# VectorE's order in the second full-attention layer: polynomial steps ahead of side-matmul reads

## The chip, the cores and the metric

The kernel runs on one core of one Trainium2 chip. The metric is the device time of one execution in microseconds (us). The engines that matter here are TensorE (PE in the profile, with PEld for its weight loads), VectorE (DVE), ScalarE (ACT), GpSimd (POOL) and the DMA queue that SyncE (SP) feeds. Each engine works through its own instruction list in order; the lists are tied together by semaphores. In this kernel the lists of TensorE, and in the full layers that of VectorE as well, are written out by hand: the program that builds the kernel decides which instruction stands behind which.

## The reference

Four transformer-like attention blocks follow each other on one sequence of 2048 rows of 512 numbers, with 32 heads of 16: a sliding-window block (window 256), a full block, the same window block again and the same full block again. Each block is

```
x = x + softmax(mask(q k^T / 4)) v  @ wo        with  q, k, v = layernorm(x) @ wqkv
```

The window blocks mask all but the last 256 keys; the full blocks mask nothing, so 32 heads x 2048 x 2048 exponentials are needed in each. The input `x` and the weights are float32 random numbers, scaled by 0.05. The kernel computes this in float32 quality: matrix products are made of float16 pieces (high and low part), and a path of higher safety, which does not run for these inputs, stands behind a flag.

## The kernel before

**Layers.** The layers are numbered 0 to 3. Layers 0 and 2 are window layers, 1 and 3 the full ones. The change concerns layer 3, the second full layer.

**Visits.** A full layer is worked in 32 *visits*. One visit takes four heads (`qd`) and 512 queries (`c`), and goes through the 2048 keys in 16 tiles of 128 keys (`attn_full`, L845). For each tile there are two score matmul sets (L789), one for each pair of heads, each into a bank pair `s` of the accumulator memory (PSUM; two such tiles exist). ScalarE takes the exponential of 1024 columns at once (L801) into `e`, and TensorE multiplies by the values into `acc` (L865), a tile later. In layer 3 the visits come in 16 *groups* of two: a group is one set of 512 queries (`c`) with eight heads (`t`), so `qd = 2t` and then `2t + 1`. In this text visits are counted from 0 to 31, so odd visits are the second ones of their groups.

**VectorE's own exponentials.** In layer 3, VectorE takes a share: in tile 5 (`OWN_J`, L40) of every visit, one of the two heads of each pair is not given to ScalarE (which then runs the half-size form, L798) but to VectorE (`own_exp`, L758). VectorE reads the scores at once (L763, two reads in a visit) and then needs seven further steps for each read: two integer operations (L766, L767) and five of a polynomial (L769). These fourteen steps have no fixed place. They are put in the last of five queues, `VQ[4]`, and go out when the program finds time. When all are out, the value products that need them, the *late halves* (`late`, L871: two sets of TensorE matmuls with `op` as an operand, each over half of the queries), may be issued, one half per tile (L1162), as soon as the planner's clock has passed the modelled end of the last step by 1.0. If the visit's last tile comes before that, both are put behind the last tile's own value product (L880). After it the epilogue (L721) reads `acc`, and the next visit's value products may overwrite it.

**Side work.** Between the tiles stands work that other visits and the layer's end need, the *side work*: projections of queries and keys (`project`, read by VectorE into `j`, L523 and the lines behind), value projections (`vt`), and the output projection (`wo_part`, L703, where VectorE adds two bank halves onto `x`, L717). All side matmuls of a full layer write one bank pair `b`, so the next side matmul must wait until VectorE has read the last. For the bound of the softmax the program also needs sums of squares: GpSimd squares the projection (`sq`, L537), TensorE sums them over a head with a matmul with ones (`squares`, L551; matmul at L559) into the same bank `b`, and VectorE reads that into `m` (queries, L593 and L594) or `km` (keys, L578). Squares that are still owed stand in the list `pend`, and `settle` (L609) issues those whose time has come; it may issue two in a row.

**What sets the order.** While it writes the lists, the program keeps a clock of TensorE (`clock`) and one of VectorE (`vt_`), both in estimated us. `soon` puts VectorE's operations that need no fixed place into the queues `VQ[0]` to `VQ[4]`. `drain` takes from the first queue that has something, as long as VectorE's clock is no more than 0.2 ahead of TensorE's. The fifth queue is skipped when squares are owed, the bank is not in the middle of a product, and the squares can go within 0.9: this is the *hold-back*. `drain(1)` empties only the first queue. `share` (L1053), called for each tile, first looks whether squares may be issued: TensorE's clock must have passed the time they are due, the time at which the bank is free (`PH["free"]`), and VectorE's clock less 0.2. Then it issues side matmuls from a budget. After a side product the bank is called free 2.0 after its last matmul, and the same after squares. A late half puts `PH["free"]` 0.1 past the clock, so that the tile it stands in gets no side matmuls.

```
            if pend and not PH["busy"] and clock[0] >= max(PH["free"], pend[0][0], vt_[0] - 0.2):
                settle(False)
                PH["free"] = clock[0] + 2.0
```

Of the kernel before, what the change touches and what calls it, by code (L numbers as in the profile page):

```python
# [193 lines left out]
def fast_path(ctx, tc, flag, a_x, a_wqkv, a_wo, b_wqkv, b_wo, out):  # L194
# [20 lines left out]
    XC, XN, V, O, OT, KM, PH = {}, {}, {}, {}, {}, {}, {"free": 0.0, "busy": False, "late": None}  # L215
    WT, ST, pend = {}, {}, []
    VQ, vt_ = [deque() for _ in range(5)], [0.0]

    clock, DONE, XNR, ONR = [0.0], {}, {}, {}
# [9 lines left out]
    def vec(us):  # L229

        vt_[0] = max(vt_[0], clock[0]) + us
# [8 lines left out]
    def drain(upto=None):  # L240

        if upto is not None:
            for q in VQ[:upto]:
                while q:
                    vec(q[0][1])
                    q.popleft()[2]()
            return
        while vt_[0] <= clock[0] + 0.2:
            q = next((q for q in VQ[:4 if pend and not PH["busy"] and max(pend[0][0], PH["free"]) <= clock[0] + 0.9 else 5] if q), None)
            if q is None:  # L250
                return
            vec(q[0][1])
            q.popleft()[2]()

    def turns(chain, *ops):

# [237 lines left out]
    def project(l, s, c, act, ht=None, ring=0):  # L494


        ty, n = l % 2, f"{l}_{s}_{c}" + ("" if ht is None else f"_h{ht}")
        w = weights(ty, s, n, *((0, D, 0) if ht is None else (ht * P, (ht + 1) * P, ring)))
        yield wait(8)
        xc = XC[l, c]  # L500
        if s == 0:
            dst = rows(qs[ty, c])
        elif ty == 0:
            dst = rows(kw[c])
        else:
            dst = rows(kf)[:, :, c * QC:(c + 1) * QC]
        sqs = {}
        for t in range(NHT) if ht is None else (ht,):
            ps = bank()
            w0 = t * P if ht is None else 0  # L510
            yield from mms(ps, [(w[:, k, a, w0:w0 + P], xc[:, b, k, :]) for a, b in TERMS for k in range(NC)], 2.2)
            if not PH["full"]:
                settle(not sqs)
            with tc.high_priority(HEAD_START):
                if PH["full"]:
                    drain(1)
                    j = vp.tile([P, QC], F32, name=f"j{n}_{t}", tag="j")
                    join(j, (ps[:, 0], ps[:, 1]))
                else:
                    sp = vp.tile([P, 2, QC], F16, name=f"sp{n}_{t}", tag="sp", bufs=3)  # L520
                    if act:
                        nc.scalar.activation(sp[:, 0], ps, AF.Copy, scale=1 / WS)
                    else:  # L523
                        nc.vector.tensor_scalar(sp[:, 0], ps, 1 / WS, None, op0=ALU.mult)
                    nc.vector.scalar_tensor_tensor(sp[:, 1], ps, 1 / WS, sp[:, 0], op0=ALU.mult, op1=ALU.subtract)
            full = PH["full"]

            def parts(t=t, sp=None if full else sp, j=j if full else None):
                if full:
                    sp = vp.tile([P, 2, QC], F16, name=f"sp{n}_{t}", tag="sp", bufs=3)  # L530
                    nc.vector.tensor_copy(sp[:, 0], j)  # L531
                    nc.vector.tensor_tensor(sp[:, 1], j, sp[:, 0], ALU.subtract)
                sq = vp.tile([P, QC], BF16, name=f"sq{n}_{t}", tag="sq", bufs=NHT)
                if act:
                    nc.scalar.activation(sq, sp[:, 0], AF.Square)
                else:
                    nc.gpsimd.tensor_tensor(sq, sp[:, 0], sp[:, 0], ALU.mult)  # L537
                sqs[t] = sq

                d = dst[8 * t:8 * t + 8].rearrange("h (d b) n -> (h d) b n", b=4)  # L540
                if s:
                    nc.sync.dma_start(d[:, 0:2], sp[:, 0:1].broadcast_to([P, 2, QC]))
                    nc.sync.dma_start(d[:, 2], sp[:, 1])
                else:
                    nc.sync.dma_start(d[:, 0:2], sp)
                    nc.sync.dma_start(d[:, 2], sp[:, 0])
            soon(0, 1.2, parts)
            yield last(MM)
        return sqs

    def squares(n, sqs):  # L551

        drain(1)
        vec(1.4)
        ph = bank()
        for t, sq in sqs.items():
            if PH["full"]:
                for r in range(2):
                    nc.tensor.matmul(ph[32 * t:32 * t + 32, r], hsum[R * r:R * r + R], sq[R * r:R * r + R],  # L559
                                     start=True, stop=True, skip_group_check=True)  # L560
            else:
                nc.tensor.matmul(ph[32 * t:32 * t + 32, :], hsum, sq, start=True, stop=True, skip_group_check=True)
        return ph

    def quarters(ht):
# [137 lines left out]
    def wo_part(c, t):  # L703

        w = wp.tile([P, NC, 2, D], F16, name=f"wo_{c}_{t}", tag="w", bufs=WB)[:, 0]
        nc.sync.dma_start(w, wd[1, 3][:, t])
        xs = load_x(3, c)
        yield wait(4)
        o = O.pop((3, c, t))
        for i in range(4):  # L710
            ps = bank()
            yield from mms(ps, [(o[:, a, i * P:(i + 1) * P], w[:, b, :]) for a, b in TERMS])
            vec(1.4)
            k = 4 * c + i
            with tc.high_priority(HEAD_START):
                for p in ((ps[:, 0], ps[:, 1]) if PH["full"] else (ps,)):
                    nc.vector.scalar_tensor_tensor(xs[i], p, 1 / WS, xs[i], op0=ALU.mult, op1=ALU.add)  # L717
            nc.sync.dma_start(out[0, k * P:(k + 1) * P, :] if t == NHT - 1 else xd[k], xs[i])
            yield -MM
# [266 lines left out]
    class Side:  # L986
# [66 lines left out]
        def share(self):  # L1053

            self.budget = min(self.budget + max((self.cost - self.spent) / max(self.steps - 3 - self.k, 1), self.least), 0.75)
            self.lag = max(self.lag - 0.42, -0.3)
            if pend and not PH["busy"] and clock[0] >= max(PH["free"], pend[0][0], vt_[0] - 0.2):
                settle(False)
                PH["free"] = clock[0] + 2.0
                self.lag += 0.1  # L1060
            s0, most = self.spent, 2.5 * MM if self.more and self.lag < -0.2 and self.budget > 0.7 else 1.5 * MM
            while (self.q and clock[0] >= PH["free"] and self.budget >= MM / 2 and (self.lag < 0.25 or self.budget > 0.45)
                   and self.spent - s0 < most):
                c = self.one()
                if c is None:
                    break
                self.budget -= abs(c)
                self.lag += abs(c)
# [324 lines left out]
```

## Time and profile before

| | |
|---|---|
| median of 3 runs | 2710.74 us (2704.07, 2710.74, 2710.8) |
| the profiled execution | 2705.62 us |
| its span, first to last instruction | 2703.4 us |
| layer 3, from its first exponential to its last | 1711.55 to 2683.3 us |
| ScalarE busy in the whole span | 2350.0 us (87%) |
| TensorE busy in the whole span (its ends are modelled) | 2490.6 us (92%) |
| VectorE busy in the whole span | 1436.0 us (53%) |
| granted clock of TensorE | 0.99 |

The profile is one execution. Its views name an instruction by its line in the kernel, the engine, and the tiles as `out<-in`. In a timeline each row gives the start and the length in us, and in brackets how long the engine had been idle before it and what ended that. A row with `x2` stands for two instructions of one kind in a row. The view of waits sums such idle times: who waited, for whom, us in total, how often, and the longest. `op` is the name of VectorE's exponentials in the late halves, and also that of a tile of the epilogue.

### The profile page before, as it was taken

The page shows a single profiled execution, that of the slowest core. Times are in us where ns is not written, and L with a number is a line of the kernel's source. Part 1 is how long each engine was busy: PE and PEld are TensorE (multiplying, and loading weights), DVE is VectorE, ACT ScalarE, POOL GpSimd, SP SyncE. Part 2 cuts the span into 40 slices and gives each one's busy share as a digit, 9 for nine tenths or more (in the row PEclk, how much of TensorE's full clock was granted, in tenths as well). Part 3 has the DMA queues.
Part 4 walks back from the last instruction along what each step waited for, and adds up shares of the span by engine and source line. Part 5 has one row for each costly group of instructions (what it writes and reads, how often), then busy time and mean ns, then how long its engine had stood idle before and what let it go on. Part 6 is the DMA issues. An engine that isn't in the chain of part 4 may idle for free.

```text
span 2703.4 us, 124036 instructions
## 1 busy us (share of the span) xinstructions
PE 2490.6 (92%) x56047; PEld 1164.5 (43%) x56047; DVE 1436.0 (53%) x2862; ACT 2350.0 (87%) x2671; POOL 549.7 (20%) x1136
## 2 busy tenths in 40 slices
PE   7889999999998999999999999889999999999997
PEld 3344444444443444444444444434444444444442
DVE  5576353223334335334336666466656676677675
ACT  4666765999999999999996775789999999999996
POOL 1556550001000000100116786010000001100000
PEclk9999999999999999999999999999999999999999
DMA  8899875222334325224326656423333333334332
GB/s 282 251 276 267 236 201 150 67 95 91 104 99 120 100 85 153 93 87 114 97 88 206 189 164 168 119 85 105 97 92 96 96 95 111 104 97 133 129 118 93
DMA packets 341204, 361.49 MB, mean 134 GB/s; under 512 B 117800, under 2 KB 256568, under 8 KB 334392
## 3 DMA queue, kind: packets, MB, share of 16 engines
q1 hardware_dynamic: 340664, 353.46, 43.9%
q8 instruction: 440, 7.21, 1.1%
q14 instruction: 100, 0.82, 0.1%
HBM read 240.65 MB, written 96.99 MB: 125 GB/s over the span
## 4 chain that ended last, share of the span: by engine, by line
ACT 51%; PE 28%; issue 11%; DVE 6%; DMA 2%; POOL 1%; SPq 1%; ACTq 0%; DVEq 0%; POOLq 0%
ACT e L801 50%; PE b L409 8%; PE acc L865 5%; PE acc L914 4%; PE s L789 4%; PE s L793 2%; PE b L405 2%; PE bs L412 2%; PE b L412 2%; DMA kt<-kw 1%; DVE xh L464 1%; POOL e L907 0%; DVE xn L458 0%; ACT e L798 0%; DVE xh L458 0%
## 5 line engine op out<-in xcount | busy, mean ns | idle before, releaser
L801 ACT ACTIVATE e<-s 128x1024 f32<-128x1024 f32 (+2 forms) x2368 | 2193.1, 1046 | 165.9 <-PE s L793 104.6
L865 PE MATMUL acc<-e,vt 64*17 64x512 f32 (+1 forms) x17152 | 1112.3, 566 | 0.7 <-issue 0.4
L789 PE MATMUL s<-qt,kt 64*32 64x512 f16 x16384 | 884.5, 381 | 121.4 <-ACT e L801 97.3
L789 PEld LDWEIGHTS <-kt 64*32 64x32 f16 x16384 | 403.5, 89 | 887.3 <-issue 787.6
L865 PEld LDWEIGHTS acc<-e,vt 64*17 64x17 f32 x17152 | 303.5, 92 | 78.1 <-issue 9.3
L907 POOL TENSOR_SCALAR_AFFINE_SELECT e<-e 128x256 f32<-128x256 f32 x512 | 231.2, 459 | 153.5 <-ACT e L801 152.8
L904 POOL TENSOR_SCALAR_AFFINE_SELECT e<-e 128x256 f32<-128x256 f32 x448 | 200.8, 454 | 98.4 <-ACT e L801 95.1
L914 PE MATMUL acc<-e,vt 128*17 128x384 f32 (+2 forms) x2816 | 201.5, 388 | 2.0 <-POOL e L904 1.7
L431 DVE TENSOR_SCALAR sa<-acc 128x512 f32<-128x512 f32 x64 | 44.2, 691 | 287.9 <-PE acc L865 287.9
L409 PE MATMUL b<-xc,w 128*32 128x512 f16 x2496 | 154.5, 392 | 11.8 <-DVE km L578 6.7
L537 POOL TENSOR_TENSOR sq<-sp 128x512 bf16<-128x512 f16 x32 | 45.8, 1434 | 505.3 <-DVE sp L531 482.1
L793 PE MATMUL s<-qt,kt 64*128 64x384 f16 (+2 forms) x1408 | 120.5, 275 | 27.1 <-ACT e L801 21.2
L769 DVE SCALAR_TENSOR_TENSOR op<-op,ou 128x512 f32<-128x512 f32 x192 | 133.4, 695 | 5.8
L431 DVE TENSOR_SCALAR j<-b 128x512 f32<-128x512 f32 x32 | 22.0, 688 | 203.5 <-PE b L405 203.5
L405 PE MATMUL b<-xc,w 64*32 64x512 f16 x3072 | 127.5, 376 | 1.5 <-DVE j L432 0.8
L537 POOL TENSOR_TENSOR sq_h<-sp_h 128x512 bf16<-128x512 f16 x29 | 44.6, 1537 | 395.1 <-DVE sp_h L531 387.2
L850 POOL TENSOR_SCALAR vh<-vt 128x17 f32<-128x17 f32 x64 | 15.5, 264 | 524.1 <-PE acc L865 503.1
L405 PE MATMUL b<-xc,w_h 64*32 64x512 f16 x2784 | 119.6, 376 | 0.4 <-issue 0.2
L752 POOL TENSOR_TENSOR oh<-o,oh 128x512 f16<-128x512 f32 x31 | 37.2, 1201 | 376.9 <-DVE oh L751 373.3
L409 PEld LDWEIGHTS <-w 128*32 128x32 f16 x2496 | 78.4, 99 | 75.1 <-issue 27.5
L431 DVE TENSOR_SCALAR vt<-b 128x256 f32<-128x256 f32 (+1 forms) x36 | 18.4, 511 | 173.5 <-PE b L405 159.1
L405 PE MATMUL b<-wo,oh 64*32 64x512 f16 x2592 | 106.8, 376 | 4.1 <-DVE m_None L594 1.8
(152 smaller groups left out, 2380.2 us busy)
## 6 DMA issues: line engine op xcount, KB each, us to landing
kt<-kf SPq DMA_DIRECT2D x128, 512.0 KB
qt<-qs SPq DMA_DIRECT2D x128, 256.0 KB
xd<-x SPq DMA_DIRECT2D x96, 256.0 KB
x<-xd SPq DMA_DIRECT2D x96, 256.0 KB
w<-wd SPq DMA_DIRECT2D x21, 1024.0 KB
kt<-kw SPq DMA_DIRECT2D x64, 256.0 KB
qs<-sp SPq DMA_DIRECT2D x48, 256.0 KB
wo<-wd SPq DMA_DIRECT2D x12, 1024.0 KB
```

The costliest lines, as they stand in the source:

```text
L405: nc.tensor.matmul(ps[g:g + 32, r], a[k, g:g + 32], b[k], start=(i == 0), stop=(i == len(pairs) - 1), skip_group_check=True)
L409: nc.tensor.matmul(ps[g:g + 32], a[:, g:g + 32], b, start=(i == 0), stop=(i == len(pairs) - 1), skip_group_check=True)
L412: nc.tensor.matmul(ps, a, b, start=(i == 0), stop=(i == len(pairs) - 1))
L537: nc.gpsimd.tensor_tensor(sq, sp[:, 0], sp[:, 0], ALU.mult)
L769: ops.append((0.7, lambda i=i, k=k: nc.vector.scalar_tensor_tensor(p, p if i else u, k / 4.0 ** (i + 1), e if i == 4 else u, op0=ALU.add, ...
L789: nc.tensor.matmul(ps[g:g + 32, h], kt[R * h:R * h + R, pr, kc + g:kc + g + 32], qt[R * h:R * h + R, pr], start=True, stop=True, skip_grou ...
L793: nc.tensor.matmul(ps[:, h, s0:s0 + wd_], kt[R * h:R * h + R, pr, kc:kc + P], qt[R * h:R * h + R, pr, qc:qc + wd_], start=True, stop=True)
L801: nc.scalar.activation(e[:, :, w0:w1], ps[:, :, w0:w1], AF.Exp, scale=SCALE)
L865: nc.tensor.matmul(acc[r][32 * h:32 * h + DH + 1, cs], v[k], e[k, cs], start=(j == 0), stop=last_, skip_group_check=True)
L904: nc.gpsimd.affine_select(v, v, pattern=[[0, 2], [-1, P]], compare_op=ALU.is_gt, fill=0.0, base=0, channel_multiplier=1)
L907: nc.gpsimd.affine_select(v, v, pattern=[[0, 2], [1, P]], compare_op=ALU.is_ge, fill=0.0, base=0, channel_multiplier=-1)
L914: nc.tensor.matmul(a[32 * h:32 * h + DH + 1, q * P:(q + nb) * P], V[l, (4 * c + j) // 4][:, j % 4, 4 * qd + h, :], es_[h // 2][:, h % 2, s ...
```

## The change

Three edits. `drain` no longer skips the fifth queue. A new function `between` issues one polynomial step, if there is one and VectorE's clock is at most 1.2 ahead of TensorE's; it is called in `project` ahead of the read of the bank, in `wo_part` ahead of the two reads, and at the end of `squares`. And `share` lets squares go when VectorE's clock is up to 1.0 ahead as long as polynomial steps are queued, where it was 0.2.

```diff
         while vt_[0] <= clock[0] + 0.2:
-            q = next((q for q in VQ[:4 if pend and not PH["busy"] and max(pend[0][0], PH["free"]) <= clock[0] + 0.9 else 5] if q), None)
+            q = next((q for q in VQ if q), None)
             if q is None:
                 return
             vec(q[0][1])
             q.popleft()[2]()
+
+    def between():
+
+        if VQ[4] and vt_[0] <= clock[0] + 1.2:
+            vec(VQ[4][0][1])
+            VQ[4].popleft()[2]()
...
                 if PH["full"]:
                     drain(1)
+                    between()
                     j = vp.tile([P, QC], F32, name=f"j{n}_{t}", tag="j")
                     join(j, (ps[:, 0], ps[:, 1]))
...
                 nc.tensor.matmul(ph[32 * t:32 * t + 32, :], hsum, sq, start=True, stop=True, skip_group_check=True)
+        between()
         return ph
...
             yield from mms(ps, [(o[:, a, i * P:(i + 1) * P], w[:, b, :]) for a, b in TERMS])
+            between()
             vec(1.4)
...
-            if pend and not PH["busy"] and clock[0] >= max(PH["free"], pend[0][0], vt_[0] - 0.2):
+            if pend and not PH["busy"] and clock[0] >= max(PH["free"], pend[0][0], vt_[0] - (1.0 if VQ[4] else 0.2)):
                 settle(False)
                 PH["free"] = clock[0] + 2.0
                 self.lag += 0.1
```

## The prediction, made before the changed kernel had run

> **What bounds the kernel now.** I read the page first, then its rows for the second full layer alone. The columns of a group are line, engine, operation, tiles, count, busy time and mean ns, and then the idle time ahead with what ended it.
>
> ```profile
> PE 2490.6 (92%) x56047; PEld 1164.5 (43%) x56047; DVE 1436.0 (53%) x2862; ACT 2350.0 (87%) x2671; POOL 549.7 (20%) x1136
> ```
>
> ```profile
> L801 ACT ACTIVATE e<-s 128x1024 f32<-128x1024 f32 x931 | 869.5, 1048 | 35.5 <-PE s L789 19.5 <-PE acc L865 12.3
> L798 ACT ACTIVATE e<-s 128x512 f32<-128x512 f32 x62 | 38.0, 612 | 3.0
> ```
>
> The second fence holds visits 1 to 31 of the layer (1742 to 2684 us; a visit is four heads by 512 queries; two visits make a group, odd ones end it). ScalarE's exponentials fill 907.5 of 942 us there. VectorE's order can therefore earn only part of the 35 us in which ScalarE idles. The two visits of one group as stretches (us, then the busy time of PE, PEld, DVE, ACT and POOL), and ScalarE's own timeline show where the idle time stands:
>
> ```profile
> 2265.27:2295.47 30.20, 28.68 (x752) 13.57 (x737) 21.66 (x36) 29.09 (x33) 3.78 (x6) 1.00 0.43 129
> 2295.47:2324.57 29.10, 26.55 (x674) 11.78 (x660) 19.77 (x34) 28.88 (x33) 1.54 (x1) 1.00 0.30 89
> ```
>
> ```profile
> 2327.44 7.48 ACT L801 ACTIVATE e<-s 128x1024 f32<-128x1024 f32 x8 [0.91 <-PE acc L865]
> ...
> 2566.09 7.48 ACT L801 ACTIVATE e<-s 128x1024 f32<-128x1024 f32 x8 [0.41 <-PE acc L865]
> ```
>
> Each first visit of a group lasts 1.10 us longer than a second one, and ScalarE stops once in it, at its start, until TensorE is through with matmuls into acc. TensorE's timeline tells which:
>
> ```profile
> 2292.44 0.60 PE L865 MATMUL acc<-op,vh 64*17 64x256 f32 x8
> 2294.17 0.60 PE L865 MATMUL acc<-op,vh 64*17 64x256 f32 x8
> ...
> 2326.06 0.39 PE L865 MATMUL acc<-op,vh 64*17 64x256 f32 x4
> ...
> 2562.45 0.60 PE L865 MATMUL acc<-op,vh 64*17 64x256 f32 x8
> 2565.15 0.39 PE L865 MATMUL acc<-op,vh 64*17 64x256 f32 x4
> ```
>
> These are the late halves: the two value products that need VectorE's own exponentials (op). In the visit from 2265 they stand one tile apart in mid-visit, and no stop follows. In the visit from 2295 both are issued after the last tile (from 2326.06 on, past the visit's 2324.57), and the stop is 0.91. In the visit to 2563.7 one is in time and one at the end, and the stop is 0.41. So a half that is not ready by the last tile costs ScalarE about 0.43 us, and the 12.3 us of "PE acc" are 15 such boundaries, 13 with two halves and 2 with one.
>
> **Why they are late.** VectorE, from its two reads of scores (L763) in that second visit:
>
> ```profile
> 2304.94 1.28 DVE L763 TENSOR_SCALAR ou<-s 128x512 int32<-128x512 f32 x2
> 2307.42 0.69 DVE L593 TENSOR_SCALAR m<-b 32x512 f16<-32x512 f32 x1 [1.20 <-PE b L559]
> ...
> 2308.86 0.43 DVE L766 TENSOR_SCALAR oe<-ou 128x512 int32<-128x512 int32 x1
> ...
> 2312.69 0.69 DVE L769 SCALAR_TENSOR_TENSOR op<-op,oe 128x512 f32<-128x512 f32 x1
> 2316.37 1.23 DVE L578 TENSOR_REDUCE km<-b 32x1 f32<-32x1024 f32 x1 [2.99 <-PE b L559]
> ...
> 2320.49 1.42 DVE L717 SCALAR_TENSOR_TENSOR x<-b,x 128x512 f32<-128x512 f32 x2 [0.52 <-PE b L405]
> ...
> 2323.27 0.69 DVE L769 SCALAR_TENSOR_TENSOR op<-op,oe 128x512 f32<-128x512 f32 x1
> ```
>
> Fourteen polynomial steps wait in VQ[4]. Four of them are 0.46 and ten 0.72 us apart, 9.04 us in all, but they take from 2306.22 to 2323.96. In between VectorE reads m, km and x (1.41 + 1.23 + 1.42) and idles 1.20 + 2.99 + 0.52 with steps in the queue. The first two idles are the hold-back of drain(): steps keep off while the squares (L559) are about to be issued.
>
> **The change part by part.**
>
> *Nothing is added.* Every instruction, DMA and queue outside VectorE's and TensorE's orders stays as it is. VQ[4] is empty outside the second full layer, where all the edits do nothing.
>
> *drain() without the hold-back, share() letting squares go with up to 1.0 us queued on VectorE.* The steps fill the idles of 1.20 and 2.99: 4.19 us. The last step ends at 2323.96 - 4.19 = 2319.8, or at 2318.4 if it then also passes ahead of the x read (1.42), that is 22.9 to 24.3 us into the visit. In the visit from 2265 the halves came 1.1 and 2.8 us after the last step (2291.35, from the 1.53 us row below). So they would stand at about 2321 and 2323 and leave the end of the visit at 2324.57.
>
> *between().* In front of the j read (L523) and the x read (L717), a step goes if VectorE's modelled queue is at most 1.2 us. That delays the bank's read by 0.72 less the idle ahead of it (0.52 above; 27.4/60 = 0.46 for the mean pair of x reads by the group below). The third call, at the end of squares(), can never act: vec(1.4) has just put the queue 1.4 past the clock, over the bound of 1.2. So the read of squares gets no step by design, only what drain() left.
>
> ```profile
> L717 DVE SCALAR_TENSOR_TENSOR x<-b,x 128x512 f32<-128x512 f32 x120 | 82.4, 687 | 27.4 <-PE b L405 25.1
> 2323.25 0.84 PE L405 MATMUL b<-wo,oh 64*32 64x512 f16 x24
> PE s L789 <- ACT e L801: 55.5, 166, 1.0
> PE b L405 <- DVE x L717: 1.5, 2, 0.8
> PE b L559 <- DVE m L594: 4.6, 3, 1.6
> ```
>
> What hides the delay: TensorE hardly waits for a bank now (1.5 us after x reads in the whole layer). The next wo matmuls start 1.34 us after the x read's end (2323.25 against 2320.49 + 1.42), and the delay is some 0.26. Without that cover TensorE would still lose to its own idle first, 55.5 us in which it waits for ScalarE to free scores. I take 0 for it; the bounds are 0 and 60 pairs by 0.26 = 16 us.
>
> *Squares in pairs.* In visit 3, and alike in 5 and 7, two squares are issued at once, and the second waits for the read of the first:
>
> ```profile
> 1821.80 0.68 DVE L594 SCALAR_TENSOR_TENSOR m<-b,m 32x512 f16<-32x512 f32 x1
> ...
> 1822.53 0.39 PE L559 MATMUL b<-sq_h,hsum 64*32 64x512 bf16 x2 [1.49 <-DVE m L594]
> ...
> 1823.28 7.48 ACT L801 ACTIVATE e<-s 128x1024 f32<-128x1024 f32 x8 [1.44 <-PE s L789]
> ```
>
> A bank wait of 1.49 costs ScalarE 1.44, with nothing to hide it. A step in front of that read adds about 0.4 (0.72 less the part that runs before the squares end; bounds 0 and 1.0, the new bound in share()). Three times: +1.2 us.
>
> *The halves in mid-visit.* Each is 0.43 us of TensorE in a tile of 1.83 us. By the rows above, the visit from 2265 took them without a stop, and PH["free"] keeps side work out of those tiles. Side work thus moves two tiles later in ten visits. I charge 0.2 us of new stops to each, 2.0 in all; bounds 0 and 0.9 per visit, as at the end now.
>
> **The sum.** Ten boundaries clear fully (after visits 5 to 23): 10 x 1.10 = 11.0. Five (after 3, 25, 27, 29, 30) have three or four pairs of x reads in the way, and the last step cannot come much below 24 us. There I count half of 3 x 1.10 + 2 x 0.6, 2.3 us. Less 1.2 and 2.0, the gain is 10.1 us. The profiled execution took 2705.6 us (span 2703.4), so it would be 2695.5. The runs lie at 2704.07, 2710.74 and 2710.8, and this one beside the fast one; the middle of all four is 2708.2. I forecast **2698** for the median, between what the two clusters would give.
>
> A rule of the Trainium skill speaks against more than this. The row first:
>
> ```profile
> 2289.25 1.55 POOL L537 TENSOR_TENSOR sq_h<-sp_h 128x512 bf16<-128x512 f16 x1 [9.98 <-DVE sp_h L531]
> 2289.82 1.53 DVE L769 SCALAR_TENSOR_TENSOR op<-op,oe 128x512 f32<-128x512 f32 x1
> ```
>
> A step of 0.69 us took 1.53 beside GpSimd's square. "SBUF — State Buffer", section "SBUF: two separate sides", says that a VectorE operation with two SBUF inputs and a GpSimd operation that reads SBUF exclude each other for a whole instruction; the trace agrees (the step ended 0.55 after GpSimd's 2290.80). By that rule a step put ahead of a bank read could hold it 1.5 instead of 0.7, past the 1.34 of margin; with 27 squares in the layer (15 m and 12 km reads), at 0.2 each, the sum would be 5 us worse, 2703. I don't take it, since GpSimd squares right behind a j read, and the step that it met here was the last of its visit, with no bank read behind it.
>
> **The rivals.** *No measurable change (0.28).* The halves are released by the planner's own clock (the last step's modelled end + 1.0, one half per tile), not by VectorE. For it: in visit 25 the last step ended at 2500.45 and both halves still stood at the end.
>
> ```profile
> 2499.76 0.69 DVE L769 SCALAR_TENSOR_TENSOR op<-op,oe 128x512 f32<-128x512 f32 x1
> 2505.72 0.39 PE L865 MATMUL acc<-op,vh 64*17 64x256 f32 x4
> ```
>
> That is 5.3 us after the last step, where I count on 2.8. If half of the ten boundaries behave like this, or if side work pushed later has to be forced at group ends, 5 us are left: 2700.6 by the profiled run, 2705 by the runs.
>
> *Slower (0.12): the bank's wait replaces the late halves.* Squares now go out with VectorE up to 1.0 us behind, while the planner calls the bank free 2.0 us after them. The read needs 1.41, so the next matmul can meet a bank in use, at the price of the 1.44 above where another square follows at once. It decides when more than (13.3 + 8.1)/1.44 = 15 of the layer's 27 squares meet this; with 18, 26 us stand against 13.3, 2718 by the profiled run, 2721 by the runs. Against it: in the visit from 2295 the bank's next users came some 7 us after the m read's end (km, 2316.37 against 2308.83) and 2 us after the km read's (x, 2320.49 less its 0.84 of matmuls, against 2317.60).
>
> **How the numbers follow.** The forecast has 0.60. About 0.3%, 8.1 us, is what a measurement here can tell from no change, which puts the limit at 2702.6. Nine tenths of the forecast's cases lie below it and a tenth of the first rival's: 0.57 faster. The slower rival gives 0.12, the rest is 0.31. The range runs from 2690 (all 15.5 us of 13 x 1.10 + 2 x 0.6 gained by the fast cluster) to 2711, the first rival in the slow cluster; most of the last rival is left out.
>
> **What would show it.** Right: the "PE acc" wait of ScalarE falls from 12.3 to 3 or less; odd visits end VectorE's last step 22 to 24 us in; late halves come in groups of eight, not four; first visits last about 29.2. Wrong: halves still at the end with the last step early (first rival), or waits of TensorE for m, km or x several times the 4.6 and 1.5 (second rival). A change before 1711 us would contradict the reading that nothing outside the layer moves.

## The result, and the profile after

The changed kernel took 2728.32 us (median of 4 runs, 2726.35 to 2729.83) against 2709.34 us for the kernel before (4 runs, 2704.07 to 2710.8). The ratio is **1.0073**, 95% interval 1.0056 to 1.0091: slower, where 2698 and a gain had been forecast. The profiled execution took 2729.83 us. Its page and its waits follow (engine, line, tile, whom it waited for: us in total, times, longest), first of the kernel after from 1730 to 2708 us, which takes in part of the first visit and the first 6.7 us behind the layer, then of the kernel before from 1742 to 2684 us. Lines have moved by 6 to 9 (the exponentials from L801 to L810, the value product from L865 to L874, side matmuls from L405 to L411).

```profile
PE 2500.4 (92%) x56047; PEld 1164.1 (43%) x56047; DVE 1428.7 (52%) x2862; ACT 2351.1 (86%) x2671; POOL 549.3 (20%) x1136
```

```profile
ACT e L810 <- PE s L798: 36.6, 22, 6.2
PE s L798 <- DMA qt<-qs: 13.3, 3, 5.2
ACT e L810 <- PE acc L874: 9.7, 11, 1.7
PE b L411 <- DVE x L726: 4.6, 4, 1.5
PE b L566 <- DVE m L602: 4.6, 3, 1.6
```

```profile
ACT e L801 <- PE s L789: 19.5, 18, 5.8
ACT e L801 <- PE acc L865: 12.3, 15, 0.9
PE s L789 <- DMA qt<-qs: 3.8, 1, 3.8
```

Every engine did the same number of instructions, and ScalarE and VectorE were busy about as long as before. The wait on `acc`, which the change was to remove, fell by only 2.6 us. Counted from 1730 us in both kernels, the wait on the scores rose from 20.5 to 36.6, by 16.1, and 13.3 us of TensorE waiting for the DMA of the queries, `qt<-qs`, stand behind it where there were 3.8.

**Where the time went.** Layer 3 is cut here at its first and its last exponential:

| us | until the first | first to last | behind the last | span |
|---|---|---|---|---|
| before | 1711.6 | 971.8 | 20.1 | 2703.4 |
| after | 1714.8 | 986.5 | 26.3 | 2727.6 |

The first column is no part of the change. Up to there all the kernels of this case have one instruction order, and over their thirteen profiled executions it lay anywhere between 1704.6 and 1714.8. Inside the layer single executions differ less, but they do: the first group of two visits took between 66.0 and 68.3 us in five kernels that have the same order there. A difference of 2 or 3 us between two profiled executions says nothing. What is left is 14.7 us inside the layer and 6.2 behind it. Most of the 14.7 is at two places. As stretches, first of the kernel before and then after, stand visits 15 and 16 and visits 23 and 24 (us, us long, busy time of PE, PEld, DVE, ACT, POOL, then the granted clock):

```profile
2176.76:2236.18 59.42, 56.28 (x1556) 27.35 (x1540) 40.84 (x71) 58.04 (x66) 5.33 (x7) 1.00 0.32 97
2414.69:2474.16 59.47, 54.97 (x1388) 24.97 (x1372) 41.95 (x71) 58.03 (x65) 5.29 (x7) 1.00 0.35 106
```

```profile
2183.51:2251.07 67.56, 59.04 (x1548) 27.70 (x1540) 39.89 (x71) 58.16 (x65) 5.32 (x7) 0.95 0.28 85
2429.08:2494.10 65.02, 57.05 (x1404) 25.71 (x1396) 41.33 (x72) 58.20 (x65) 5.33 (x7) 0.97 0.32 97
```

They grew by 8.14 and 5.55, 13.7 of the 14.7. ScalarE's timeline at the start of visit 16 shows the first of the two. The kernel before has a single stop there, of 0.91:

```profile
2208.85 3.77 ACT L801 ACTIVATE e<-s 128x1024 f32<-128x1024 f32 x4 [0.91 <-PE acc L865]
```

The kernel after has three in a row:

```profile
2218.93 1.02 ACT L810 ACTIVATE e<-s 128x1024 f32<-128x1024 f32 x1 [6.16 <-PE s L798]
2221.06 1.02 ACT L810 ACTIVATE e<-s 128x1024 f32<-128x1024 f32 x1 [1.11 <-PE s L798]
2223.82 2.86 ACT L810 ACTIVATE e<-s 128x1024 f32<-128x1024 f32 x3 [1.73 <-PE acc L874]
```

**The chain to this stop** begins a visit earlier. In visit 14 (2153.25 to 2183.51) VectorE is through with its steps at 2175.74, 22.5 us into the visit; before it was 2172.64, 26.2 us into a visit that began at 2146.42. VectorE's last step of that visit, and TensorE's side work and late halves in visits 14 and 15, before:

```profile
2171.11 1.53 DVE L769 SCALAR_TENSOR_TENSOR op<-op,oe 128x512 f32<-128x512 f32 x1
```

```profile
2171.77 0.84 PE L405 MATMUL b<-xc,w_h 64*32 64x512 f16 x24
2173.73 0.60 PE L865 MATMUL acc<-op,vh 64*17 64x256 f32 x8
2175.45 0.60 PE L865 MATMUL acc<-op,vh 64*17 64x256 f32 x8
...
2182.96 0.63 PE L405 MATMUL b<-xc,w_h 64*32 64x512 f16 x16
...
2188.28 0.38 PE L559 MATMUL b<-sq_h,hsum 64*32 64x512 bf16 x2
...
2199.06 0.38 PE L559 MATMUL b<-sq_h,hsum 64*32 64x512 bf16 x2
```

and the same after, with VectorE's step and then TensorE's row at which the queries are waited for:

```profile
2175.05 0.69 DVE L778 SCALAR_TENSOR_TENSOR op<-op,oe 128x512 f32<-128x512 f32 x1
```

```profile
2178.62 0.60 PE L874 MATMUL acc<-op,vh 64*17 64x256 f32 x8
2180.45 0.60 PE L874 MATMUL acc<-op,vh 64*17 64x256 f32 x8
2182.27 0.84 PE L411 MATMUL b<-xc,w_h 64*32 64x512 f16 x24
...
2195.09 0.41 PE L411 MATMUL b<-xc,w_h 64*32 64x512 f16 x8
2198.67 0.39 PE L566 MATMUL b<-sq_h,hsum 64*32 64x512 bf16 x2
...
2209.55 0.38 PE L566 MATMUL b<-sq_h,hsum 64*32 64x512 bf16 x2
2211.44 1.50 PE L411 MATMUL b<-wv,xc 64*32 64x256 f16 x96
...
2218.18 0.63 PE L798 MATMUL s<-qt,kt 64*32 64x512 f16 x8 [5.24 <-DMA qt<-qs]
```

Counted from the start of each visit:

| | before | after |
|---|---|---|
| late halves of visit 14 | 27.3 and 29.0 | 25.4 and 27.2 |
| first 24 matmuls of the next projection | 25.3 | 29.0 |
| last matmuls of that projection, in visit 15 | 6.2 (x16) | 11.6 (x8) |
| squares for the keys and for the queries, visit 15 | 11.5 and 22.3 | 15.2 and 26.0 |

The steps of the first visit end earlier, so the late halves stand one tile earlier, and each closes its tile to side work. The projection's first 24 matmuls lose their place and go two tiles later. In visit 15, eight matmuls of it no longer fit ahead of VectorE's own tile and wait until 11.6. Squares come 3.7 us later. The m of the queries is written so late that its DMA issue follows at 2211.41, and the load of the next visit's queries behind it, at 2212.83. The same two of the kernel before come first:

```profile
2200.92 0.29 SPq L606 DMA_DIRECT2D qs<-m  x1
2202.29 0.87 SPq L822 DMA_DIRECT2D qt<-qs  x2
```

```profile
2211.41 0.29 SPq L614 DMA_DIRECT2D qs<-m  x1
2211.75 0.36 SPq L840 DMA_DIRECT2D kt<-kf  x1
2212.83 0.87 SPq L831 DMA_DIRECT2D qt<-qs  x2
```

The load is there for TensorE at 2218.18, 5.35 us after its issue. Before, TensorE began visit 16's scores at 2205.30, 3.0 us after the issue, and no stop on the scores followed. So two things add up to the stop: counted from the visit's start the load is issued 3.8 later, and it takes 2.3 longer. Ahead of it now stands a load of 512 KB of keys (`kt<-kf`, 2211.75), which before was issued 2.5 us behind it. That the two loads share the DMA engines, whose busy share was 0.95 to 1.02 in each us from 2214 to 2217, would explain the 2.3; no run separates it.

From visit 9 to 23 the squares come later in every second visit, but only visits 16 and 24 wait for the load. In visits 15 and 23 the keys' squares go first, and the queries' m is read last, 26.5 and 24.7 us into the visit. In the other second visits from 9 to 21 it is the queries' m that comes first, at 16.4, and then the load is in time. The 96 matmuls of a value projection in one go (2211.44) are what had not found room before the visit ended.

### The profile page after: what moved, and what is told of

Same layout as the page of the kernel before. It is cut to its first block, busy times and chain, and to the rows that moved or that the text cites. A ratio compares the mean times of both kernels' runs of the same rounds, so it can differ in the third digit from the quotient of the medians.

```text
span 2727.6 us, 124048 instructions
## 1 busy us (share of the span) xinstructions
PE 2500.4 (92%) x56047; PEld 1164.1 (43%) x56047; DVE 1428.7 (52%) x2862; ACT 2351.1 (86%) x2671; POOL 549.3 (20%) x1136
## 4 chain that ended last, share of the span: by engine, by line
ACT 51%; PE 29%; issue 11%; DVE 6%; DMA 3%; SPq 0%; POOL 0%; ACTq 0%; DVEq 0%; POOLq 0%
ACT e L810 49%; PE b L415 7%; PE acc L874 5%; PE acc L923 4%; PE s L798 4%; PE b L411 2%; PE s L802 2%; PE bs L418 2%; PE b L418 2%; DMA x<-in_A_x_dram 1%; ACT e L807 1%; DMA qt<-qs 1%; DVE xh L470 1%; DVE xn L464 0%; DVE xh L464 0%
## 5 line engine op out<-in xcount | busy, mean ns | idle before, releaser
L810 ACT ACTIVATE e<-s 128x1024 f32<-128x1024 f32 (+2 forms) x2368 | 2194.2, 1047 | 181.5 <-PE s L802 105.4
L874 PE MATMUL acc<-e,vt 64*17 64x512 f32 (+1 forms) x17152 | 1113.5, 567 | 0.4 <-issue 0.3
L874 PEld LDWEIGHTS acc<-e,vt 64*17 64x17 f32 x17152 | 303.3, 93 | 79.7 <-issue 11.6
L802 PE MATMUL s<-qt,kt 64*128 64x384 f16 (+2 forms) x1408 | 121.0, 277 | 27.0 <-ACT e L810 20.2
L411 PE MATMUL b<-xc,w 64*32 64x512 f16 x3072 | 127.5, 376 | 1.5 <-DVE j L438 0.8
L411 PE MATMUL b<-xc,w_h 64*32 64x512 f16 x2784 | 119.7, 376 | 0.2 <-issue 0.2
L411 PE MATMUL b<-wo,oh 64*32 64x512 f16 x2592 | 106.1, 376 | 7.2 <-DVE x L726 4.6
L415 PEld LDWEIGHTS <-w 128*32 128x32 f16 x2496 | 75.3, 99 | 77.8 <-issue 26.8
L859 POOL TENSOR_SCALAR vh<-vt 128x17 f32<-128x17 f32 x64 | 15.5, 263 | 460.2 <-PE acc L874 439.1
```

Of the source, the lines that this page charges most:

```text
L411: nc.tensor.matmul(ps[g:g + 32, r], a[k, g:g + 32], b[k], start=(i == 0), stop=(i == len(pairs) - 1), skip_group_check=True)
L415: nc.tensor.matmul(ps[g:g + 32], a[:, g:g + 32], b, start=(i == 0), stop=(i == len(pairs) - 1), skip_group_check=True)
L802: nc.tensor.matmul(ps[:, h, s0:s0 + wd_], kt[R * h:R * h + R, pr, kc:kc + P], qt[R * h:R * h + R, pr, qc:qc + wd_], start=True, stop=True)
L810: nc.scalar.activation(e[:, :, w0:w1], ps[:, :, w0:w1], AF.Exp, scale=SCALE)
L874: nc.tensor.matmul(acc[r][32 * h:32 * h + DH + 1, cs], v[k], e[k, cs], start=(j == 0), stop=last_, skip_group_check=True)
```

## The experiments

**Which part does it.** The three edits were tried apart. The kernel before was run again beside each set of experiments, with medians from 2704.49 to 2707.72 us, and each ratio is against those of its own set. The third alone (the bound of 1.0 for squares) gives the same instruction order as the kernel before, so it has no run.

`between()` alone:

```diff
+    def between():
+        if VQ[4] and vt_[0] <= clock[0] + 1.2:
+            vec(VQ[4][0][1])
+            VQ[4].popleft()[2]()
...
                     drain(1)
+                    between()
...
+        between()
         return ph
...
+            between()
             vec(1.4)
```

> The kernel before with between() alone: hold-back and squares' condition as before. Displaced projection: the first visits' late halves move up one tile, and the next projection's first step moves from tile 13 to 15, so the squares of queries are later, but the second squares of a visit stay at tile 11 or 12, so few group ends wait: 2708 to 2718, with more output products left for the layer's end. Bank waits: the steps ahead of reads are all there, so the whole loss: 2720 to 2730.

Measured: 2723.47 us (6 runs) against 2707.19, ratio 1.0055 [1.0038, 1.0072]. The layer from first to last exponential is 985.2 us, 13.4 longer than before, and the tail behind it 27.4. So this edit alone carries most of the loss. The time by itself speaks for the rival: it lies in the range given for bank waits, above that for the displaced projection. What decides is where the time went. Visits 15 and 16 last 35.63 and 31.95 us, as in the kernel after, the queries' m of visit 15 is read 26.6 us into it (22.7 before), and TensorE waits 4.21 us for the queries' load. Its waits for VectorE at the bank add up to 15.0 us in the layer, where they were 9.0, so up to 6 us of the loss may be theirs. Visits 23 and 24, 29.48 and 30.26, are not hurt, and smaller stops are spread over others.

The hold-back alone taken out:

```diff
-            q = next((q for q in VQ[:4 if pend and not PH["busy"] and max(pend[0][0], PH["free"]) <= clock[0] + 0.9 else 5] if q), None)
+            q = next((q for q in VQ if q), None)
```

> The kernel before without the hold-back alone (no between(), squares' old condition). The planner's VectorE clock then stays up to 0.9 ahead while steps are queued, so squares with the bound of 0.2 wait until the steps are out: in several second visits the second squares go at tile 15 or in the next visit. Displaced squares theory: where the squares of queries come at the visit's end the next visit waits for them by DMA, 3 to 6 us in two to four groups: 2712 to 2725. Rival (only late halves at the ends count, 15 instead of 28): 2699 to 2704.

Measured: 2736.88 us (5 runs), ratio 1.0107 [1.0093, 1.0122], more than expected and worse than all three edits together. ScalarE's timeline at the start of visit 16, and TensorE's squares ahead of it:

```profile
2227.16 1.02 ACT L801 ACTIVATE e<-s 128x1024 f32<-128x1024 f32 x1 [13.60 <-PE s L789]
```

```profile
2212.60 0.38 PE L559 MATMUL b<-sq_h,hsum 64*32 64x512 bf16 x2
```

The first squares of visit 15 (from 2184.05) wait until 28.6 us into it, against 11.5, and those for the queries come right behind. Stops of 6.64, 13.60 and 11.03 us follow at the starts of visits 12, 16 and 24. Steps keep VectorE's estimated clock more than 0.2 ahead of TensorE's, and then the rule for squares, in `share`, never lets them go. The hold-back had been there for that.

The hold-back out and the bound of 1.0 in, without `between()`:

> The changed kernel without between(): only the hold-back is gone and squares may go with VectorE 1.0 behind. Both theories expect the loss to be gone. Displaced projection: first visits end their steps at tile 12 as before, so nothing moves there; second visits end theirs two tiles earlier, 7 of 28 late halves leave the ends, at 0.43 to 0.55 us each 3 to 4 us: 2703 to 2708. Bank waits: no step is put ahead of a read by design, 2700 to 2710.

Measured: 2707.21 us (11 runs), ratio 0.9998 [0.9989, 1.0007]: no change. The wait on `acc` falls to 9.2 us, the wait on the scores is 24.5 (20.5 before), and the tail grows by 3.3 to 23.4. The third edit is what makes the first one harmless, and the first alone gains nothing that lasts.

**Is it the first visits?** If the chain above is right, the late halves of first visits are at fault and not VectorE's steps. The changed kernel with these halves kept off the tiles before the visit's last but one:

```diff
-                    elif PH["late"] and PH["late"][0].get("left") == 0 and PH["late"][0]["done"] + 1.0 <= clock[0]:
+                    elif PH["late"] and PH["late"][0].get("left") == 0 and PH["late"][0]["done"] + 1.0 <= clock[0] and (qd % 2 or u >= NT - 2):
```

> The changed kernel, but in the first visit of each group a late half may not go before tile 14, where the kernel before put it. Theory (displaced projection: the earlier late halves of first visits push the first step of the next projection from tile 13 to 15, its last step then misses the tiles ahead of VectorE's own tile in the second visit, squares come 3.7 us later, and groups end with waits for queries): the waits of 3 to 6 us at group ends are gone, the squares of second visits are read near 12 and 21 us again, and the time is 2695 to 2707, not above the kernel before. Rival (steps ahead of bank reads make TensorE wait for the bank): the steps stand as in the changed kernel, so the time stays at 2720 to 2730.

Measured: 2711.11 us (12 runs), ratio 1.0012 [1.0002, 1.0022]. Every step of VectorE keeps its edit, and the 14.7 us are gone: the layer takes 970.6. At the start of visit 16 only the old stop stands, as in ScalarE's timeline:

```profile
2212.44 7.48 ACT L810 ACTIVATE e<-s 128x1024 f32<-128x1024 f32 x8 [0.91 <-PE acc L874]
```

What it still loses is the tail, 26.8 us, which the expectation had not counted: the time lies above its range.

The kernel before with no edit to VectorE's steps, but two tiles of each first visit are closed to side work, at the place that late halves take after the change:

```diff
+                    if l == 3 and qd % 2 == 0 and u in (NT - 3, NT - 2):
+                        PH["free"] = max(PH["free"], clock[0] + 0.1)
                     sd.step()
```

> The kernel before, with one thing added: in the first visit of each group of the second full layer tiles 13 and 14 take no side matmuls. No polynomial step moves by design. Theory (displaced projection): this alone brings the loss, squares in second visits near 15 and 24 us, waits of 3 us or more at several group ends, 2718 to 2735. Rival (bank waits from the moved steps): no step is moved, so 2705 to 2712 as before.

Measured: 2728.11 us (6 runs) against 2707.19, ratio 1.0077 [1.0061, 1.0092], the loss of the change itself: in the profiled execution 13.6 us in the layer (985.4) and 5.4 in the tail (25.5). VectorE is through with the steps of visit 14 at 26.2 us, as before. The projection's first 24 matmuls go to visit 15, 1.7 us into it, where before they stood in visit 14; that is later than in the kernel after, since here the late halves keep their old places and close the visit's last tile as well. Its last 24 wait until 11.5 us into visit 15, and the stops at the start of visit 16 are those of the kernel after:

```profile
2206.65 1.02 ACT L801 ACTIVATE e<-s 128x1024 f32<-128x1024 f32 x1 [6.06 <-PE s L789]
...
2211.36 1.94 ACT L801 ACTIVATE e<-s 128x1024 f32<-128x1024 f32 x2 [1.55 <-PE acc L865]
```

Closing two tiles is thus enough for the loss, and moving the halves back is enough to remove what is lost inside the layer.

The same from the other side: the changed kernel in which `between()` acts in second visits alone.

```diff
-        if VQ[4] and vt_[0] <= clock[0] + 1.2:
+        if VQ[4] and PH["second"] and vt_[0] <= clock[0] + 1.2:
...
+            PH["second"] = l == 3 and qd % 2
```

> The changed kernel with between() active in the second visits of the groups alone; in first visits the steps then end at tile 12 as before, and the next projection's first step stands at tile 13. Theory (the loss comes from the first visits' steps ending a tile earlier): the waits of 3 to 6 us at group ends are gone, 17 of 28 late halves stay at ends, 5 to 6 us gained in the layer's body, three output products left at the end take 6 back: 2703 to 2709, like the kernel before. Rival (steps ahead of bank reads cost in second visits, where most of them stand): 2715 or more.

Measured: 2709.48 us (11 runs) against 2704.49, ratio 1.0014 [1.0005, 1.0023]. The layer takes 969.5 us, 2.3 less than before, which is within what single executions differ by, and the tail of 26.7 gives more back.

**What the two terms are worth.** First the tail. In the kernel after, three output products find no tile in visit 31; two of them start after the last exponential, which ends at 2701.26. TensorE after:

```profile
2702.62 0.84 PE L411 MATMUL b<-wo,oh 64*32 64x512 f16 x24 [1.54 <-DVE x L726]
2705.00 0.84 PE L411 MATMUL b<-wo,oh 64*32 64x512 f16 x24 [1.54 <-DVE x L726]
```

The kernel before with three such products left for the end: side work is kept off all but the first tiles of the last visit.

```diff
+                    if l == 3 and not after and u >= 2:
+                        PH["free"] = max(PH["free"], clock[0] + 0.1)
                     sd.step()
```

> The kernel before, with the last visit's tiles from 2 on closed to side matmuls, so that three output products (nine steps) that it does at tiles 2, 6 and 8 are left for the end of the layer, as many as the changed kernel leaves there. Theory (leftover at the end): each is a product of 0.65 us and a bank read of 1.4 with nothing beside it, some 2.1 us, so the layer's body stays and the time from the last exponential to the end grows from 20 to 26 us: 2713 to 2717. Rival (the end has room, since the last epilogue and the output matmuls wait for VectorE anyway): within 2 us of the kernel before.

Measured: 2714.16 us (9 runs) against 2705.5, ratio 1.0023 [1.0010, 1.0037]. The tail is 26.7 us against 20.1, 6.6 for three products. Two of them follow each other at 2.4 us in the rows above, since each has to wait until VectorE has read the bank that it shares with the one ahead. The last visit itself, freed of the three, is 1.2 us shorter. The 6.2 us of the change's tail, with as many products left, are explained by it.

Then what late halves at the ends cost. The kernel before without the late halves of second visits; these value products are left out, so its output lacks them:

```diff
-                    for pr, own in OWN:
+                    for pr, own in OWN if qd % 2 == 0 else ():
```

> The kernel before, with the late value products of every second visit left out (the outputs lack VectorE's share of two heads there; its polynomial steps still run, and the planner still counts the products). Theory of the prediction (a late half at a visit's end costs ScalarE 0.43 us and a little more): the stops of 0.91 at the starts of first visits vanish, and the time falls by 12 to 16 us, to 2692 to 2697. Rival (the stop has another cause at the group's end, such as the output product or the epilogue's read): it stays, and the time falls by less than 4.

Measured: 2687.87 us (6 runs), ratio 0.9932 [0.9917, 0.9948]. That is 17.6 us less, more than expected; the layer takes 956.1 us, 15.7 less. ScalarE's waits there:

```profile
ACT e L801 <- PE s L789: 17.7, 13, 6.1
ACT e L801 <- PE acc L865: 0.4, 1, 0.4
```

So the price that the prediction put on halves at the ends, 15.5 us for all of them, holds in size. As the products are left out here and not moved, it bounds what an order can gain by clearing the ends of second visits.

**Is there an order that gains?** The changed kernel, in which second visits may issue halves as soon as VectorE's last step is modelled to be through and the bank is in use anyway, while first visits hold theirs to a late tile:

```diff
-                    elif PH["late"] and PH["late"][0].get("left") == 0 and PH["late"][0]["done"] + 1.0 <= clock[0]:
+                    elif PH["late"] and PH["late"][0].get("left") == 0 and PH["late"][0]["done"] + (0.0 if qd % 2 else 1.0) <= clock[0] and (qd % 2 and (PH["free"] > clock[0] or u >= NT - 1) or qd % 2 == 0 and u >= (NT - 2 if g >= 4 else NT - 3)):
```

> The changed kernel with another rule for the late halves: in first visits not before the tile that the kernel before gave them (13, from the fifth group on 14); in second visits as soon as the last step is through by the planner, but only in a tile in which the bank is in use anyway, or the last one. The planner then leaves 13 halves at ends (28 before, 20 changed), squares of second visits stand at tiles 6 and 11 or 12 as before, and one output product is left at the end (three changed, none before). Theory (displaced side work explains the loss, and halves at the ends cost what the prediction said): 2697 to 2705, faster than both. If the moved steps themselves cost time: 2710 or more.

Measured: 2703.41 us (12 runs), ratio 0.9993 [0.9983, 1.0003]: not to be told from no change. The wait on `acc` falls to 5.6 us and the tail is 20.2, but the wait on the scores is 24.6 where it was 20.5 from 1730 us on. Of that, 2.39 is at the start of visit 10, where the kernel before had no stop and where the end of visit 9 now holds a value projection.

`after_second` with the early release (0.0 in place of 1.0) in second visits:

> As after_second, and in second visits a late half may go as soon as the planner's clock passes the modelled end of the last step (no further 1.0). The planner leaves 12 halves at ends (28 before), squares of second visits at tiles 6 and 11 or 12 as before, one output product at the end. Theory: 16 halves at 0.55 us gained, 8 to 9 us, less 2 at the end and less a little where TensorE waits for a step: 2697 to 2703, faster than both kernels. Rival (a half issued that early makes TensorE wait for VectorE, or the products it displaces are forced at group ends): 2704 or more.

Measured: 2704.82 us (11 runs), ratio 0.9999 [0.9989, 1.0010]. From group 1 on its layer is 5.8 us shorter than before (900.0 against 905.8), but group 0 takes 69.3, where five kernels with the order of the kernel before took 66.0 to 68.3: the first squares of visit 1 come 30.0 us into it and not 27.9, and ScalarE then stops for 8.2 us at the start of visit 2, not 5.8. The time lies in the rival's range.

The last one leaves group 0 and the two last groups alone. All three edits and the early release act in the second visits of groups 1 to 13, and everything else is as in the kernel before. (Its expectation names 16 groups for `between()`; in the kernel that ran, it acts in these 13.)

```diff
+            PH["second"] = l == 3 and qd % 2 and 0 < g < 14
...
-            q = next((q for q in VQ if q), None)
+            q = next((q for q in VQ[:5 if PH["second"] or not (pend and not PH["busy"] and max(pend[0][0], PH["free"]) <= clock[0] + 0.9) else 4] if q), None)
...
-        if VQ[4] and vt_[0] <= clock[0] + 1.2:
+        if VQ[4] and PH["second"] and vt_[0] <= clock[0] + 1.2:
...
-            if pend and not PH["busy"] and clock[0] >= max(PH["free"], pend[0][0], vt_[0] - (1.0 if VQ[4] else 0.2)):
+            if pend and not PH["busy"] and clock[0] >= max(PH["free"], pend[0][0], vt_[0] - (1.0 if VQ[4] and PH["second"] else 0.2)):
...
-                    elif PH["late"] and PH["late"][0].get("left") == 0 and PH["late"][0]["done"] + 1.0 <= clock[0]:
+                    elif PH["late"] and PH["late"][0].get("left") == 0 and PH["late"][0]["done"] + (0.0 if PH["second"] else 1.0) <= clock[0]:
```

> The changed kernel with two conditions: between() acts and the late halves go out as soon as the planner's clock has passed the last step's modelled end (not 1.0 later), both only in second visits (between() in all 16 groups, the earlier release in groups 1 to 13). First visits keep the order of the kernel before. In the order so written 16 late halves stand at the end of a second visit (28 in the kernel before), no output product is left for the layer's end, and group 0, where earlier halves had cost 3 us, is as before. Theory of displaced side work: 12 halves leave the ends at about 0.55 us each, 6 to 7 us, and nothing is given back: 2697 to 2702 by the median, ratio 0.997 to 0.998, tail 20 us, wait on acc about 6 us. Rival, VectorE's steps as such delay bank reads: as in the change itself, slower than before by about a third of its loss, for between() acts in second visits alone: about 1.002. If the gain is given back at other places once more, the ratio is within 0.999 to 1.001 and the wait on the scores at group starts is above 22 us.

Measured: 2702.29 us (12 runs, 2696.82 to 2708.03) against 2707.72 (17 runs, 2701.68 to 2712.89), ratio **0.9980** [0.9971, 0.9988]: faster than the kernel before and than the change. Its span was 2698.9 us, 1709.2 + 969.5 + 20.3. Late halves at the ends are down from 28 to 16 in the order as written. ScalarE's waits:

```profile
ACT e L810 <- PE s L798: 23.7, 24, 6.1
ACT e L810 <- PE acc L874: 6.3, 10, 0.9
```

It gains 6.0 on `acc` and loses 3.2 on the scores (20.5 before, counted alike from 1730 us), mostly in stops of less than 1 us. The wait on the scores is above the 22 that the expectation had named as the mark of a gain given back. That mark was too sharp: `before_tail`, with the order of the kernel before up to its last visit, waits 22.0. Inside the layer and its tail the profiled executions give 2.1 us, which is within what they differ by; the 5.4 us between the medians also hold what the executions differ by in front of layer 3. The sign is measured, for the best of three orders tried; that the layer alone gives 5.4 is not.

## Why the prediction was wrong, point by point

- **What bounds the kernel**: right. ScalarE was busy for 2351.1 us, as before, and each difference above is a stop of ScalarE or the tail. The price of halves at the ends also held in size: 15.5 us was worked out for all 28 of them (13 x 1.10 + 2 x 0.6, some 0.55 each and not the 0.43 named), and the layer got 15.7 shorter without them.
- **The steps fill VectorE's idles, and the last step ends at 22.9 to 24.3 us into second visits**: wrong for most visits. In the kernel after it ended 27.3 to 28.6 us into every second visit from 3 to 23, and 23.4 to 24.2 in 25, 27 and 29. VectorE's timeline at the end of visit 15 shows why: the last step follows the m read, and that follows the squares, which had moved from 22.3 to 26.0 us into the visit.

```profile
2209.97 0.69 DVE L601 TENSOR_SCALAR m<-b 32x512 f16<-32x512 f32 x1 [1.32 <-PE b L566]
...
2211.41 0.69 DVE L778 SCALAR_TENSOR_TENSOR op<-op,oe 128x512 f32<-128x512 f32 x1
```

  VectorE still idled (1.32 here), since the squares moved too. But the step fails without that as well. In `after_held` squares stand where they were, and the last step of visits 9 to 23 still ended 25.0 to 27.3 us into the visit. VectorE's timeline there in visit 19, the one that the prediction works out (28.5 before, 22.9 to 24.3 forecast, 27.1 here):

```profile
2310.52 0.69 DVE L601 TENSOR_SCALAR m<-b 32x512 f16<-32x512 f32 x1 [0.40 <-PE b L566]
...
2314.86 1.42 DVE L726 SCALAR_TENSOR_TENSOR x<-b,x 128x512 f32<-128x512 f32 x2
...
2319.50 1.23 DVE L586 TENSOR_REDUCE km<-b 32x1 f32<-32x1024 f32 x1 [1.83 <-PE b L566]
...
2325.00 0.68 DVE L778 SCALAR_TENSOR_TENSOR op<-op,oe 128x512 f32<-128x512 f32 x1
```

  The steps fill 2.0 of the 4.19 us of idle time (0.40 and 1.83 are left of 1.20 and 2.99), and one more pair of x reads, of an output product that had stood elsewhere, now comes ahead of the last step. The prediction counted on all of the idle time and on VectorE's other work staying as it was. In the kernel after, 20 of the 28 halves at the ends were still there, and the wait on `acc` was 9.7, where 3 or less had been named as the mark of the forecast.
- **The step that failed** and made the kernel slower is *the halves in mid-visit*: "Side work thus moves two tiles later in ten visits. I charge 0.2 us of new stops to each, 2.0 in all". It counted second visits only. The steps of first visits move as well, and there the halves already stood in mid-visit, so nothing was to be won and a projection was in the way. And it charged 0.2 as if these matmuls were only late by themselves. The projection is the head of a chain (projection, squares, m, a write, a load, the next visit's scores), and at visit 16 the chain paid 8.1 us for a move of two tiles, 13.7 with visit 24. Output products pushed past the layer's end came to 6.2 more. `before_blocked` gave the whole of it with no edit to VectorE's steps, and `after_held` took it out of the layer with all three edits in.
- **between() costs nothing at the bank**: near enough. Inside the layer TensorE waits 1.5 us after x reads, as before; of the 4.6 in the view above, 3.1 are the two waits of the tail. All its waits for VectorE at the bank in the layer add up to 11.5 us, where they were 9.0. The large stops at visits 16 and 24 are waits for a DMA.
- **The rule on a shared port**, weighed at 5 us: it did not bear on the change. VectorE's steps stretched by GpSimd (1.27 and 1.53 us) were 24 in the layer before and 14 after, and next behind none of the 14 stood a read of the bank.
- **The slower rival (a bank wait in place of the late halves)** had the sign and a size near it (2721), by another mechanism, so its nearness is luck. **The first rival** was right that halves stay at the ends, and it alone named the cause, side work pushed later and forced at group ends. But it priced this as a part of the gain lost, not as a loss, and its 2705 should read 2703 by the 2708.2 that the other sums start from.
- **"A change before 1711 us would contradict"**: the mark was set too sharp. The first exponential of layer 3 came 3.2 us later after the change, and over all profiled executions it varies by 10.2 with one instruction order.

## What to carry to other kernels

Where the order of an in-order engine is written out by a planner with fixed slots, finishing work *earlier* on another engine is not free: ask which slot the work that it releases will take, what stood in that slot, and follow the displaced work to its last user, DMAs included. Price it by that chain's margin at its end (here a load that was issued 3.6 us ahead of its visit's first exponential, 2202.29 to 2205.84, and when it was late came behind another load and needed 5.4 us, 2212.83 to 2218.18) and not by the length of the matmuls moved. Before an edit, look at the places where it acts but has nothing to win (here the first visits), and leave them out. And idle time ahead of an engine's operations is only a bound on what moving them earns: other work may take it.

## What the runs showed of the hardware

In the kernel after, a long wait of TensorE cost more than its length. Here are two windows of 1 us behind TensorE's last matmul of visit 15, which ends at 2212.94 (the granted clock is the number behind POOL's):

```profile
2215.00:2216.00 1.00, 0.00 (x0) 0.00 (x0) 0.00 (x0) 0.00 (x0) 0.00 (x0) 0.81 1.00 333
2216.00:2217.00 1.00, 0.00 (x0) 0.00 (x0) 0.00 (x0) 0.00 (x0) 0.00 (x0) 0.50 0.95 318
```

After some 3 us without a matmul the granted clock fell to 0.50. It was still 0.50 in the window from 2218 to 2222 and 0.94 in the next:

```profile
2218.00:2222.00 4.00, 3.82 (x48) 1.27 (x52) 0.00 (x0) 1.96 (x2) 0.00 (x0) 0.50 0.01 5
2222.00:2226.00 4.00, 3.65 (x93) 1.50 (x85) 2.30 (x4) 2.27 (x4) 0.48 (x2) 0.94 0.01 4
```

The set of eight score matmuls at 2218.18 took 0.63 where such a set takes 0.41 at full clock. So the stop of 6.16 was followed by 1.11 and 1.73 where 0.91 is usual, 1.9 us more, and the one of 4.27 at visit 24 by 1.11 and 1.05. The stops of 3.33 and 3.64 at visits 14 and 10 were not followed by it; there TensorE was busy with value projections, and the granted clock stayed at 1.00. The Trainium skill, "TensorE: Matmul & The Clock Gate", section "Part 1: The HAM clock gate", states half the clock after an idle window of about 3.4 us and full clock after as long a busy one. The trace agrees with the second, the rise after about 4 us of work. It agrees with the first only roughly: the fall came after 2.1 to 3.1 us of idle time (2212.94, a modelled end, to 2216), sooner than a whole such window.
